# A weight chunk's float64 words handled at 1024 columns instead of twice 512, with an instruction order worked out anew

## The chip, the cores and the metric

The kernel runs on one core of one Trainium2 chip. The metric is the device time of one execution in microseconds (us). Five engines work side by side: TensorE (PE, matrix products), VectorE (DVE), ScalarE (ACT), GpSimd (POOL) and SyncE (SP, which issues the transfers). Each takes its instructions in the order in which they stand in its own queue, and waits at an instruction until what that one reads is there.

## The reference

Linear attention with random features, then two feed-forward layers, in single precision; the weights arrive as float64.

```
# attention: batch 4, heads 8, seq 576, head_dim 64, 128 features
h   = x @ omega.T - sum(x*x)/2           # x = q*s or k*s, s = 64**-0.25
phi = exp(h - max(h)) / sqrt(128)
kv  = einsum('bhsm,bhsd->bhmd', phi(k), v);  z = sum(phi(k))
a   = (phi(q) @ kv) / (phi(q) . z + 1e-6)
# x = a as [2304 tokens, 512]
xn  = x / sqrt(mean(x*x) + 1e-6) * rms_g
g   = xn @ w_gate                        # [512, 1536]
y   = (g*sigmoid(g) * (xn @ w_val)) @ w_out     # [1536, 512]
h   = y @ w_in                           # [512, 2048]
out = where(h > 0, h, exp(min(h, 0)) - 1) @ w_out2   # [2048, 512]
```

## The kernel before

**Work and tiles.** All products in the feed-forward layers run on pairs of 16-bit numbers: each operand is split into a high and a low part, and three matmuls of 128x256 replace one. The 2304 tokens are 9 blocks of 256, and a block is two query tiles of 128 (query tiles 6 and 7 are block 3, 8 and 9 block 4). `k_job` takes one of 20 key tiles through the feature map `phi` into the sums of its batch; `q_job` takes one of 18 query tiles through `phi`, a transposing transfer, 24 small matmuls with the sums (128x65 in the trace, the attention product), the division, the norm, the split and another transposing transfer. What comes out is the tile's *x*: the right-hand operand of `moe1_pair`, whose matmuls (`RM,RW`, 128x256) can't start without it. `moe1_pair` and `moe1_out` are the first feed-forward layer of one block, `moe2_quad` and `moe2_out` the second.

**Weights.** `Conv` (line 675) brings a chunk of 128 x 1024 float64 numbers on chip and turns it into float32 with integer steps. There are 34 chunks: 6 each of wg (`w_gate`), wv (`w_val`) and wo (`w_out`), 8 of w1 (`w_in`) and 8 of w2 (the second `w_out`). `load` issues two transfers, one per half of the chunk, into raw buffers of 512 columns x 2 words. `words` makes three results out of each half: the size without its sign from the upper word (ACT, or DVE, as the planner chooses), the top bits of the lower word (POOL, or DVE), and the sign bit (always DVE, on 16-bit numbers). `fp32` then finds the largest value of the chunk over all 1024 columns at once, and for each half joins the parts with a shift-and-or (DVE). Then the chunk's largest exponent over all partitions is needed: `spread` has PE turn a column of 128 maxima into a row (a matmul `RI,RS` of 1x128), DVE reduces it, and a second small matmul (`RS,RI`) hands it to all partitions. `split` scales and splits into high and low part. `spread` is used as well for each query tile and for each block's result (*the exponent* of a tile, a block or a chunk below). For w1 `conv_cols` does this 8 times with one buffer set `cv2`; w2 goes through DRAM first (`conv_store`, then `conv_forms`). wg, wv and wo use the set `cv`, which lies in RX (the arena that later holds the first layer's results): four raw halves, four halves for the sign and low bits, and three wide results. `cv2` and w2's set have two raw halves and two of the other kind, in RA.

**The order.** Nothing is issued as it is written. A `Plan` records every instruction with a cost, works out due times backwards from the two layers' products (the *spine*, whose order on PE is given), and then places the instructions one after the other on the five engines. The queues hold what it worked out, in that order. Where a step can go to two or three engines (`plan.choose`), the cheapest by its own costs gets it. The numbers at the head of the file bend this: `BIAS` shifts the due times of one job each (0 to 37 the key and query tiles, 38 to 43 the chunks of wg and wv, 44 to 56 wo, 57 w1, 58 the store of w2, 60 its forms, 61 the second layer), `PRICE` the choice of engine, `AHEAD`, `BLIM`, `PELEAD`, `INFL`, `LEAD` and `STRETCH` how early things are taken. As `Plan` issues all, each row of the trace names line 530; rows are told apart by their tiles: RA and RX work buffers and weights under way, RW the weights of the first layer, RM x and the blocks' temporaries, RS single columns, RI the unit matrix and the ones of `spread`, ps the banks of PSUM, w the weights w1 and w2 in DRAM, f the DRAM buffers for w2.

Of the kernel before, what the change touches and what calls it, by code (L numbers as in the profile page):

```python
# [7 lines left out]
F32 = mybir.dt.float32  # L8
F16 = mybir.dt.float16
I32 = mybir.dt.int32  # L10
U32 = mybir.dt.uint32
U16 = mybir.dt.uint16
BF16 = mybir.dt.bfloat16
AF = mybir.ActivationFunctionType
ALU = mybir.AluOpType
# [9 lines left out]
TPE = 1  # L25
KV32 = 2
HALF = 2
AHEAD, BLIM = 1540580.623, 6
QPE = 3
FINE = 9  # L30
BIAS = [1, -22, 0, -12, 8, 10, 1, -7, -6, 14, 26, 7, 0, 2, -36, -40, 59, 0, 26, -23, 0, -36, 41, -65, -115, 60, 0, -2, -73, -72, 0, -47, -43, -15, 226, -101, -257, -27, 0, 11, -9, -26, 15, 25, 55, 0, 3, 53, -60, 1, -17, 1, 102, 7, 7, -1, 0, 28, -17, 3, 56, 56]
LOOK, WEIGH = 0.076, 80
PRICE = [2.561, 1.313, 0.814, 2.417, 0.6, 0.917]
PELEAD = 127543.557
INFL, LEAD = 1.668, 51.224
STRETCH = (11.923, 880.565, 0.234)
NBLK = NT // NB
EXPM = 0x7F800000
SGN = -(1 << 31)
# [100 lines left out]
class Plan:  # L140
# [7 lines left out]
    SPAN = 3.4133  # L148
    SPARE = {"B": 2, "L": 2, "M": 2}
    FIRST = range(38, 57)  # L150
# [154 lines left out]
    def deadlines(self):  # L305
        at = 0.0
        for op in self.ops:
            op.due = 1e9
            if op.spine:
                op.due = at  # L310
                at += op.cost * (STRETCH[0] if at < STRETCH[1] else STRETCH[2])
        for op in reversed(self.ops):
# [3 lines left out]
    def order(self, limit=None):  # L316
        for op in self.ops:
            op.due -= BIAS[op.job] * (not op.spine)
        left = [len(op.deps) for op in self.ops]
# [85 lines left out]
        while True:  # L405
# [134 lines left out]
def fused(ctx: ExitStack, tc: tile.TileContext, qT, kT, kTt, qn, kn, v, v1, omT, eye, g, wg, wv, wo, w1, w2, out):  # L540
    nc = tc.nc
    plan = Plan()
    vec, act, pool, pe, sp = [plan.engine(n, e) for n, e in (("DVE", nc.vector), ("ACT", nc.scalar), ("POOL", nc.gpsimd), ("PE", nc.tensor), ("SP", nc.sync))]
# [60 lines left out]
    in_r, d_r, e_r, qp_r = Dyn("L", [1024], F32), Dyn("L", [1024], F32), Dyn("L", [2, 1024], F16), Dyn("L", [16, P], F16)  # L604
    x_r, xs_r, S_r = Dyn("M", [512], F32), Dyn("M", [2, 512], F16), Dyn("M", [8, P], F16)

# [9 lines left out]
    isi, e2, so2 = tt([8]), tt([8]), tt([8])  # L616
# [58 lines left out]
    class Conv:  # L675


        def __init__(self, raw, A, M):
            self.raw = Rot([a.view(o, [512, 2], I32) for a, o in raw])
            self.A = Rot([a.view(o, [512], I32) for a, o in A])  # L680
            self.M = Rot([a.view(o, [1024], F32) for a, o in M])

        def load(self, st, src):
            st["raw"] = [self.raw.next(), self.raw.next()]
            n = src.shape[1] // 2
            for i, r in enumerate(st["raw"]):
                sp.dma_start(out=r.rearrange("p (k f) w -> p k (f w)", k=n), in_=src[:, i * n:(i + 1) * n])

        def words(self, st):


            if "M" not in st:
                st["M"] = self.M.next()
            M = st["M"]
            st["A"] = [self.A.next(), self.A.next()]
            for i, (r, A) in enumerate(zip(st["raw"], st["A"])):
                Mi = M[:, 512 * i:512 * i + 512]
                plan.choose(lambda: act.activation(out=Mi, in_=r[:, :, 1].bitcast(F32), func=AF.Abs),
                            lambda: vec.tensor_scalar(out=Mi.bitcast(I32), in0=r[:, :, 1], scalar1=0x7FFFFFFF, scalar2=None, op0=ALU.bitwise_and))
                A16 = A.bitcast(U16).rearrange("p (f w) -> p f w", w=2)  # L700
                r16 = r.rearrange("p f w -> p (f w)").bitcast(U16).rearrange("p (f w) -> p f w", w=4)
                plan.choose(lambda: pool.tensor_scalar(out=A, in0=r[:, :, 0].bitcast(U32), scalar1=2.0 ** -29 * (1.0 - 2.0 ** -10), scalar2=-0.4995, op0=ALU.mult, op1=ALU.add),
                            lambda: vec.tensor_scalar(out=A16[:, :, 0], in0=r16[:, :, 1], scalar1=13, scalar2=None, op0=ALU.logical_shift_right))
                vec.tensor_scalar(out=A16[:, :, 1], in0=r16[:, :, 3], scalar1=0x8000, scalar2=None, op0=ALU.bitwise_and)

        def fp32(self, st, mcol):

            M = st["M"]
            vec.tensor_scalar(out=M, in0=M, scalar1=65536.0, scalar2=2.0, op0=ALU.mult, op1=ALU.max, accum_out=mcol)
            for i, A in enumerate(st["A"]):  # L710
                Mi = M[:, 512 * i:512 * i + 512].bitcast(I32)
                vec.scalar_tensor_tensor(out=Mi, in0=Mi, scalar=3, in1=A, op0=ALU.logical_shift_left, op1=ALU.bitwise_or)

        def split(self, st, hi, lo, s, parts=1):

# [22 lines left out]
    def src_rows(w, j):  # L738
        return w.rearrange("(k p) f -> p k f", p=P)[:, 2 * j:2 * j + 2, :]
# [33 lines left out]
    def conv_store(cv, w, e):  # L773

        for j in range(8):
            st = {}
            cv.load(st, src_rows(w, j))
            cv.words(st)
            cv.fp32(st, e[:, j:j + 1])
            sp.dma_start(out=f2[j], in_=st["M"])  # L780
# [62 lines left out]
    def setup_consts():  # L843
        sp.dma_start(out=om[0:64], in_=omT)
        sp.dma_start(out=om2[64:128], in_=omT)
        sp.dma_start(out=idn, in_=eye)
        sp.dma_start(out=gx, in_=g.partition_broadcast(P))
        vec.tensor_scalar(out=om[0:64], in0=om[0:64], scalar1=cc, scalar2=None, op0=ALU.mult)
        vec.memset(om[64:128], -cc * cc / 2.0)
        vec.tensor_scalar(out=om2[64:128], in0=om2[64:128], scalar1=cc, scalar2=None, op0=ALU.mult)  # L850
        vec.memset(om2[0:64], -cc * cc / 2.0)
        vec.memset(mh, -0.5)
        m, m_, mg = sm(1, "m1"), sm(1, "m1b"), sm(1, "mg")
        vec.memset(m, 1e-30)
        vec.tensor_reduce(out=m[0:64], in_=om[0:64], op=ALU.max, axis=AX.X, apply_absolute_value=True)
        vec.memset(ones, 1.0)
        vec.tensor_scalar(out=m_, in0=spread(m, 1), scalar1=1e-30, scalar2=None, op0=ALU.max)
        iw = sm(1, "iw")
        s = pow2(m_, 12, iw)
        for a in (0, 64):  # L860
            act.activation(out=Wh[a:a + 64], in_=om[0:64], func=AF.Copy, scale=s[0:64])
            vec.scalar_tensor_tensor(out=Wl[a:a + 64], in0=om[0:64], scalar=s[0:64], in1=Wh[0:64], op0=ALU.mult, op1=ALU.subtract)
        vec.tensor_copy(out=kap0, in_=iw)
        vec.tensor_reduce(out=mg, in_=gx, op=ALU.max, axis=AX.X, apply_absolute_value=True)
        vec.tensor_scalar(out=mg, in0=mg, scalar1=1e-30, scalar2=None, op0=ALU.max)
        s = pow2(mg, -1, gpow)
        vec.tensor_scalar(out=gx, in0=gx, scalar1=s, scalar2=None, op0=ALU.mult)
# [457 lines left out]
        plan.job = 59  # L1325

    setup_consts()
    cv = Conv([(RX, i * 4096) for i in range(4)], [(RX, 16384 + i * 2048) for i in range(4)], [(RX, 24576 + i * 4096) for i in range(3)])

    def wo_scales():  # L1330
        ih = sm(6, "ih")
# [10 lines left out]
    for t in range(2 * NBLK):  # L1342
        if t % 2 == 0 and t // 2 >= 2:
            i = t // 2 - 2
# [21 lines left out]
        q_job(t, key)  # L1366
        plan.job = 59
        key += 1
    cv2 = Conv([(RA, 32768), (RA, 36864)], [(RA, 40960 + i * 2048) for i in range(2)], [(RA, 45056 + i * 4096) for i in range(3)])
    room = Rot([RA.view(o, [1024], F32) for o in (45056, 49152, 53248, 32768, 36864)] + [RM.view(28672, [1024], F32)])  # L1370
    plan.job = 58
    conv_store(Conv([(RA, 34816), (RA, 38912)], [(RA, 43008), (RA, 45056)], [(RA, 47104)]), w2, e2)
    plan.job = 57
    for j in range(8):
        conv_cols(cv2, [(w1, WI)], j, isi[:, j:j + 1])
# [69 lines left out]
```

## Time and profile before

| | |
|---|---|
| median of 3 runs | 987.38 us (986.22 to 987.43) |
| the profiled execution | 987.1 us |
| its span in the trace | 985.3 us |
| PE, DVE, ACT, POOL busy in the span | 93%, 67%, 55%, 63% |
| mean granted clock of PE | 0.972 of full speed |

The time is that of the whole execution, the span runs from the first to the last instruction of the trace; 1.8 us lie around it. A share of busy time is a mean over stages with different limits. So a reader looks at the stages one by one: which engine is nearly always busy there, and, where PE idles, which event ended its wait. The granted clock falls where PE has idled and rises again later, so an idle microsecond of PE can cost more than itself.

### The profile page before, as it was taken

To read this page: it belongs to the slowest core of one execution; us is meant where nothing else is said; L and a number is where in the kernel's file an instruction comes from. 1 tells how busy PE (TensorE), PEld (TensorE's weight loads), DVE (VectorE), ACT (ScalarE), POOL (GpSimd) and SP (SyncE) were. 2 spreads that over 40 slices of the span, in tenths; PEclk is the share of its full clock that TensorE was granted. 3 is DMA by queue.
4 is the path that set the end of the run, shared out by engine and by line. 5 is a ranking of instruction groups with operands and counts; after the bars stand their busy time and mean duration, and the time that the engine had idled before them with its cause. 6 is when DMAs were issued, how large, how long until landed. Compare 5 with 4: busy or idle time off the path is not lost. (4 is left out here: it accounts for less than half of the span.)

```text
span 985.3 us, 22369 instructions
## 1 busy us (share of the span) xinstructions
PE 919.1 (93%) x8904; PEld 808.2 (82%) x8904; DVE 662.1 (67%) x1618; ACT 541.7 (55%) x1014; POOL 621.6 (63%) x676
## 2 busy tenths in 40 slices
PE   6486789999989999999999999999999999999998
PEld 5386678788878878888887778888888888888887
DVE  6876899856678775768985886377626475365642
ACT  6886554625556756664643456777535564354630
POOL 2669766856969688788664568999515264152630
PEclk9587899999999999999999999999999999999999
DMA  9954554123331252124765433100000000000001
GB/s 260 231 155 142 161 173 169 28 55 87 76 87 55 66 108 71 33 77 140 187 220 130 137 120 108 65 1 7 12 23 12 12 12 17 18 17 12 12 12 43
DMA packets 82567, 82.57 MB, mean 84 GB/s; under 512 B 52896, under 2 KB 57888, under 8 KB 82464
## 3 DMA queue, kind: packets, MB, share of 16 engines
q1 hardware_dynamic: 82464, 81.16, 29.6%
q8 instruction: 69, 1.13, 0.5%
q14 instruction: 34, 0.28, 0.1%
HBM read 59.90 MB, written 8.91 MB: 70 GB/s over the span
## 5 line engine op out<-in xcount | busy, mean ns | idle before, releaser
L530 PEld LDWEIGHTS <-RW 128*128 128x128 f16 x4864 | 457.7, 99 | 79.3 <-issue 16.4
L530 PE MATMUL ps<-RM,RW 128*128 128x256 f16 (+1 forms) x3240 | 369.1, 272 | 5.7 <-POOL RW L530 2.4
L530 PEld LDWEIGHTS <-RA 128*128 128x128 f16 (+2 forms) x2984 | 257.6, 98 | 33.5 <-issue 3.6
L530 PE MATMUL ps<-RX,RA 128*128 128x256 f16 x1728 | 196.3, 273 | 1.3 <-DVE RM L530 1.2
L530 POOL TENSOR_TENSOR RA<-RA 64x512 f16<-64x512 f32 (+4 forms) x108 | 144.9, 1343 | 40.0 <-ACT RA L530 14.5
L530 ACT ACTIVATE RM<-ps,RC 128x512 f32<-128x512 f32 (+1 forms) x135 | 90.0, 669 | 103.1 <-PE ps L530 66.4
L530 ACT ACTIVATE RM<-RM 128x512 f32<-128x512 f32 (+3 forms) x166 | 98.1, 594 | 39.2 <-DVE RM L530 34.3
L530 DVE SCALAR_TENSOR_TENSOR ps<-ps,RM 128x512 f32<-128x512 f32 x72 | 50.2, 697 | 91.7 <-POOL RM L530 91.6
L530 POOL TENSOR_SCALAR RM<-RM,RC 128x512 f32<-128x512 f32 x72 | 55.3, 768 | 84.9 <-ACT RM L530 84.4
L530 POOL TENSOR_TENSOR RM<-RM 128x512 f16<-128x512 f32 (+1 forms) x97 | 95.7, 994 | 12.5 <-ACT RM L530 6.6
L530 DVE TENSOR_REDUCE RS<-ps 128x4 f32<-128x512 f32 (+5 forms) x146 | 75.0, 536 | 36.4 <-PE ps L530 36.0
L530 PE MATMUL ps<-RX,RW 128*128 128x256 f16 x864 | 98.5, 273 | 0.2 <-DVE RA L530 0.2
L530 ACT ACTIVATE RA<-RA 128x512 f32<-128x512 f32 (+3 forms) x88 | 66.7, 769 | 56.3 <-DVE RA L530 19.9
L530 DVE SCALAR_TENSOR_TENSOR RM<-RM,ps 128x512 f32<-128x512 f32 x108 | 73.0, 680 | 36.2 <-ACT RM L530 25.0
L530 POOL TENSOR_TENSOR RW<-RM,RW 128x256 f16<-128x256 f32 (+1 forms) x67 | 48.1, 727 | 39.3 <-ACT RW L530 24.8
L530 PE MATMUL ps<-RW 128*128 128x256 f16 x600 | 71.7, 273 | 0.9 <-DVE RM L530 0.9
L530 ACT ACTIVATE RA<-RA,RS 64x512 f16<-64x512 f32 (+3 forms) x71 | 53.0, 758 | 29.9 <-POOL RS L530 19.5
L530 PE MATMUL ps<-RW,RA 128*128 128x256 f16 (+2 forms) x560 | 67.0, 273 | 1.2 <-DVE RM L530 1.2
L530 POOL TENSOR_SCALAR RA<-RA,RS 64x512 f32<-64x512 f32 (+3 forms) x67 | 48.3, 721 | 24.9 <-ACT RA L530 21.4
L530 DVE TENSOR_TENSOR RM<-ps,RM 128x256 f32<-128x256 f32 x108 | 45.0, 420 | 10.5 <-ACT RM L530 6.2
L530 POOL TENSOR_SCALAR RX<-RX 128x512 int32<-128x512 uint32 x36 | 26.7, 742 | 40.1 <-DMA RX<-wg 13.9
L530 DVE SCALAR_TENSOR_TENSOR RM<-ps,RC,RM 128x256 f32<-128x256 f32 x54 | 25.1, 478 | 39.6 <-PE ps L530 35.7
(143 smaller groups left out, 1194.7 us busy)
## 6 DMA issues: line engine op xcount, KB each, us to landing
RA<-w SPq DMA_DIRECT2D x32, 512.0 KB, 4.0
RX<-wg SPq DMA_DIRECT2D x12, 512.0 KB, 5.2
RX<-wv SPq DMA_DIRECT2D x12, 512.0 KB, 6.0
RX<-wo SPq DMA_DIRECT2D x12, 512.0 KB, 4.9
out<-RM SPq DMA_DIRECT2D x36, 128.0 KB, 1.7
f<-RA SPq DMA_DIRECT2D x8, 512.0 KB, 3.0
RA<-f SPq DMA_DIRECT2D x8, 512.0 KB, 3.3
RA<-qn SPq DMA_DIRECT2D x11, 256.0 KB, 3.0
```

The lines of the kernel that those rows point to most:

```text
L530: getattr(real, fn)(*[fix(x) for x in a], **{i: fix(x) for i, x in k.items()})
```

## The change

`Conv` no longer works in halves. A raw buffer holds 1024 columns x 2 words, and each step of `words` and the shift-and-or of `fp32` is one instruction over 1024 columns. The transfers stay two of half a chunk each, into one buffer. The bytes of the buffers stay the same: `cv` now has two whole raw buffers and two whole ones of the other kind, `cv2` and w2's set one of each.

```diff
-AHEAD, BLIM = 1540580.623, 6
+AHEAD, BLIM = 2665473.472, 7
...
-PRICE = [2.561, 1.313, 0.814, 2.417, 0.6, 0.917]
+PRICE = [2.61, 1.246, 0.912, 2.233, 0.537, 1.098]
...
-            self.raw = Rot([a.view(o, [512, 2], I32) for a, o in raw])
-            self.A = Rot([a.view(o, [512], I32) for a, o in A])
+            self.raw = Rot([a.view(o, [1024, 2], I32) for a, o in raw])
+            self.A = Rot([a.view(o, [1024], I32) for a, o in A])
...
-            st["raw"] = [self.raw.next(), self.raw.next()]
-            n = src.shape[1] // 2
-            for i, r in enumerate(st["raw"]):
-                sp.dma_start(out=r.rearrange("p (k f) w -> p k (f w)", k=n), in_=src[:, i * n:(i + 1) * n])
+            st["raw"] = self.raw.next()
+            n = src.shape[1]
+            r = st["raw"].rearrange("p (k f) w -> p k (f w)", k=n)
+            for i in range(2):
+                c = slice(i * n // 2, (i + 1) * n // 2)
+                sp.dma_start(out=r[:, c], in_=src[:, c])
...
-            st["A"] = [self.A.next(), self.A.next()]
-            for i, (r, A) in enumerate(zip(st["raw"], st["A"])):
-                Mi = M[:, 512 * i:512 * i + 512]
-                plan.choose(lambda: act.activation(out=Mi, in_=r[:, :, 1].bitcast(F32), func=AF.Abs),
...
+            M, r = st["M"], st["raw"]
+            A = st["A"] = self.A.next()
+            plan.choose(lambda: act.activation(out=M, in_=r[:, :, 1].bitcast(F32), func=AF.Abs),
...
-            for i, A in enumerate(st["A"]):
-                Mi = M[:, 512 * i:512 * i + 512].bitcast(I32)
-                vec.scalar_tensor_tensor(out=Mi, in0=Mi, scalar=3, in1=A, op0=ALU.logical_shift_left, op1=ALU.bitwise_or)
+            Mi = M.bitcast(I32)
+            vec.scalar_tensor_tensor(out=Mi, in0=Mi, scalar=3, in1=st["A"], op0=ALU.logical_shift_left, op1=ALU.bitwise_or)
...
-    cv = Conv([(RX, i * 4096) for i in range(4)], [(RX, 16384 + i * 2048) for i in range(4)], [(RX, 24576 + i * 4096) for i in range(3)])
+    cv = Conv([(RX, i * 8192) for i in range(2)], [(RX, 16384 + i * 4096) for i in range(2)], [(RX, 24576 + i * 4096) for i in range(3)])
...
-    cv2 = Conv([(RA, 32768), (RA, 36864)], [(RA, 40960 + i * 2048) for i in range(2)], [(RA, 45056 + i * 4096) for i in range(3)])
+    cv2 = Conv([(RA, 32768)], [(RA, 40960)], [(RA, 45056 + i * 4096) for i in range(3)])
...
-    conv_store(Conv([(RA, 34816), (RA, 38912)], [(RA, 43008), (RA, 45056)], [(RA, 47104)]), w2, e2)
+    conv_store(Conv([(RA, 34816)], [(RA, 43008)], [(RA, 47104)]), w2, e2)
```

All the other numbers of the planner change too, nearly every one of `BIAS`. In the instruction streams DVE has 1536 instructions where it had 1584, ACT 962 where it had 995, POOL 613 where it had 672, and PE the same 8696. DVE has 263 to 276 `tensor_tensor`, since 13 subtractions went there from POOL. PE's order differs in the first half and is nearly the same from the second layer on.

The head of SP's queue before, where kT is the first key tiles, omT the attention's omega and qT the first query tile:

```order
L530 DMA RW<-kT 64x1024
L530 DMA RO<-omT 64x128
L530 DMA RC<-omT 64x128
L530 DMA RW<-kTt 64x512
L530 DMA RW<-kT 64x1024
L530 DMA RX<-wg 128x2x512 x2
L530 DMA RX<-wv 128x2x512 x2
L530 DMA RI<-eye 128x128
```

And now:

```order
L530 DMA RX<-wg 128x2x512 x2
L530 DMA RX<-wv 128x2x512 x2
L530 DMA RW<-kT 64x1024
L530 DMA RO<-omT 64x128
L530 DMA RC<-omT 64x128
L530 DMA RW<-kTt 64x512
L530 DMA RI<-eye 128x128
L530 DMA RW<-qT 64x1024
```

The four transfers of the first wg and wv chunk moved ahead of the first key tile.

PE's queue before, where block 2's exponent is made (the two small matmuls) and the first product on block 3's x follows (the last row):

```order
L530 LDWEIGHTS RS
L530 MATMUL ps_65<-RI,RS 1x128
L530 LDWEIGHTS RI
L530 MATMUL ps_65<-RS,RI 128x1
L530 LDWEIGHTS RW
L530 MATMUL ps_68<-RM,RW 128x256
```

And now, the first small matmul with what stands around it:

```order
L530 MATMUL ps_62<-RM,RW 128x256
L530 LDWEIGHTS RS
L530 MATMUL ps_61<-RI,RS 1x128
L530 LDWEIGHTS RW
L530 MATMUL ps_62<-RM,RW 128x256
```

The second one stands 24 matmuls later. Between query tile 7's attention product and the first matmul on its x there stood 68 matmuls before, and 424 stand there now; for tile 9 these are 116 and 124.

SP's queue before, where the w1 and w2 chunks are loaded (`RA<-w`; the store of the last w2 chunk is `f_83<-RA`, and the transposes are those of late query tiles' x):

```order
L530 DMA RA<-w 128x2x512
L530 DMA f_83<-RA 128x1024
L530 DMA RA<-w 128x2x512
L530 DMA_TRANSPOSE RX<-RA 128x8x128
L530 DMA RA<-w 128x2x512
L530 DMA_TRANSPOSE RX<-RA 128x8x128
L530 DMA RA<-w 128x2x512 x13
```

And now:

```order
L530 DMA f_82<-RA 128x1024
L530 DMA_TRANSPOSE RX<-RA 128x8x128 x2
L530 DMA RA<-w 128x2x512
L530 DMA f_83<-RA 128x1024
L530 DMA_TRANSPOSE RX<-RA 128x8x128
L530 DMA RA<-w 128x2x512 x15
```

The loads of w1 stand behind the transposes now and follow one another. Between the small matmuls for the first and for the last of w1's eight exponents PE had 412 matmuls before and has 494 now.

## Rows read from the trace of the kernel before

**Rows 1.** Page: each engine's busy time, share of the span and instructions.

```profile
PE 919.1 (93%) x8904; PEld 808.2 (82%) x8904; DVE 662.1 (67%) x1618; ACT 541.7 (55%) x1014; POOL 621.6 (63%) x676
```

**Rows 2.** Stretches: length; PE, PEld, DVE, ACT, POOL busy (instructions); clock; DMA share, GB/s.

```profile
0.00:60.00 60.00, 35.01 (x219) 31.23 (x220) 41.71 (x114) 44.86 (x80) 29.30 (x37) 0.77 0.78 210
60.00:125.00 65.00, 48.95 (x526) 44.36 (x525) 52.25 (x140) 40.65 (x78) 52.48 (x58) 0.84 0.60 173
125.00:205.00 80.00, 74.14 (x740) 64.27 (x738) 70.59 (x135) 43.15 (x66) 59.06 (x52) 1.00 0.39 114
275.00:291.00 16.00, 12.61 (x123) 10.02 (x121) 11.29 (x39) 8.77 (x13) 11.54 (x10) 0.89 0.33 72
345.00:354.00 9.00, 7.04 (x72) 5.61 (x70) 6.59 (x26) 3.95 (x7) 7.71 (x9) 0.81 0.34 65
526.00:593.00 67.00, 61.01 (x538) 50.78 (x536) 51.96 (x138) 30.09 (x43) 38.77 (x36) 1.00 0.47 131
```

**Rows 3.** Chain of waits, its last long piece: start, length, what.

```profile
915.10 67.00 PE ps L530 x612
```

**Rows 4.** Groups by form: out<-in, count; busy us, mean ns; idle before and releasers.

```profile
L530 ACT ACTIVATE RX<-RX 128x512 f32<-128x512 f32 x27 | 18.1, 670 | 9.0 <-POOL RW L530 4.7 <-DMA RX<-wg 2.4 <-DMA RX<-wv 1.8
L530 ACT ACTIVATE RA<-RA 128x1024 f32<-128x1024 f32 x6 | 6.3, 1056 | 9.2 <-DVE RA L530 9.2
L530 DVE SCALAR_TENSOR_TENSOR RM<-RM,ps 128x512 f32<-128x512 f32 x108 | 73.0, 680 | 36.2 <-ACT RM L530 25.0 <-PE ps L530 10.2
L530 DVE SCALAR_TENSOR_TENSOR RM<-ps,RM 128x256 f32<-128x256 f32 x36 | 15.2, 423 | 1.1
L530 DVE TENSOR_SCALAR RA<-RA 128x512 uint16<-128x512 uint16 x32 | 18.2, 573 | 6.5 <-POOL RA L530 6.5
L530 DVE SCALAR_TENSOR_TENSOR RA<-RA 128x512 int32<-128x512 int32 x32 | 24.7, 803 | 0.2
L530 POOL TENSOR_SCALAR RA<-RA 128x512 int32<-128x512 uint32 x32 | 25.1, 785 | 35.9 <-DMA RA<-w 21.4 <-DVE RA L530 11.6 <-POOL RA L530 0.7
```

**Rows 5.** Timeline, 0 to 10 us: start, length, engine, instruction [idle before <-releaser].

```profile
3.90 1.10 SPq L530 DMA_DIRECT2D RX<-wg  x2
...
5.12 5.26 PE L530 MATMUL ps<-RO,RW 128*128 128x128 f32 x22 [5.12 <-ACT RW L530]
...
8.60 0.65 POOL L530 TENSOR_SCALAR RX<-RX 128x512 int32<-128x512 uint32 x1 [8.17 <-DMA RX<-wg]
...
9.28 0.46 DVE L530 TENSOR_SCALAR RX<-RX 128x512 uint16<-128x512 uint16 x1 [4.32 <-POOL RX L530]
```

**Rows 6.** Timeline, 272 to 290 us, PE and SP's queue, tile 7 and block 3.

```profile
272.35 0.90 PE L530 MATMUL ps<-RA,RX 128*128 128x65 f16 x24
...
280.43 1.23 SPq L530 DMA_TRANSPOSE RM<-RA  x1
280.82 0.22 PE L530 MATMUL ps<-RI,RS 128*1 128x128 f16 x1 [0.97 <-DVE RS L530]
...
283.62 1.99 PE L530 MATMUL ps<-RM,RW 128*128 128x256 f16 x12 [2.05 <-DMA RM<-RA]
```

**Rows 7.** Timeline, 345 to 353 us, PE, around block 3's exponent.

```profile
347.90 0.16 PE L530 MATMUL ps<-RS,RI 1*128 1x1 bf16 x1 [1.05 <-DVE RS L530]
...
349.16 1.61 PE L530 MATMUL ps<-RO,RA 128*128 128x128 f16 x14 [0.88 <-POOL RA L530]
```

**Rows 8.** Page: DMA issues of w1, w2 (KB, us to landing); timeline, w1's stage.

```profile
RA<-w SPq DMA_DIRECT2D x32, 512.0 KB, 4.0
...
538.32 0.22 PE L530 MATMUL ps<-RI,RS 128*1 128x128 f16 x1 [2.23 <-DVE RA L530]
...
559.05 1.12 POOL L530 TENSOR_SCALAR RA<-RA,RS 128x1024 f32<-128x1024 f32 x1 [3.54 <-ACT RA L530]
560.25 2.13 POOL L530 TENSOR_TENSOR RA<-RA 128x1024 f16<-128x1024 f32 x1
...
589.28 0.22 PE L530 MATMUL ps<-RI,RS 128*1 128x128 f16 x1 [0.63 <-DVE RA L530]
```

More of the change, by code (lines that the diff above doesn't have):

```diff
@@ L27 @@
 HALF = 2
-AHEAD, BLIM = 1540580.623, 6
+AHEAD, BLIM = 2665473.472, 7
 QPE = 3
 FINE = 9
-BIAS = [1, -22, 0, -12, 8, 10, 1, -7, -6, 14, 26, 7, 0, 2, -36, -40, 59, 0, 26, -23, 0, -36, 41, -65, -115, 60, 0, -2, -73, -72, 0, -47, -43, -15, 226, -101, -257, -27, 0, 11, -9, -26, 15, 25, 55, 0, 3, 53, -60, 1, -17, 1, 102, 7, 7, -1, 0, 28, -17, 3, 56, 56]
+BIAS = [0, -24, -6, -13, 9, 11, 1, -18, 4, 16, 26, 0, 3, 0, -42, -66, 48, 0, 24, -36, 11, -47, 60, -76, -82, 71, 3, 7, -74, -72, 7, -40, -68, -29, 214, -138, -2, -19, 6, 12, -10, -26, 30, 98, 29, -5, -6, 50, -58, 0, -29, 29, 0, 7, -28, 113, -9, 8, -23, 3, 1, 0]
 LOOK, WEIGH = 0.076, 80
-PRICE = [2.561, 1.313, 0.814, 2.417, 0.6, 0.917]
-PELEAD = 127543.557
-INFL, LEAD = 1.668, 51.224
-STRETCH = (11.923, 880.565, 0.234)
+PRICE = [2.61, 1.246, 0.912, 2.233, 0.537, 1.098]
+PELEAD = 228143.172
+INFL, LEAD = 1.815, 51.617
+STRETCH = (11.046, 890.942, 0.188)
 NBLK = NT // NB
@@ L693, in words @@
                 st["M"] = self.M.next()
-            M = st["M"]
-            st["A"] = [self.A.next(), self.A.next()]
-            for i, (r, A) in enumerate(zip(st["raw"], st["A"])):
-                Mi = M[:, 512 * i:512 * i + 512]
-                plan.choose(lambda: act.activation(out=Mi, in_=r[:, :, 1].bitcast(F32), func=AF.Abs),
[L699 to L704, printed above, removed]
+            M, r = st["M"], st["raw"]
+            A = st["A"] = self.A.next()
+            plan.choose(lambda: act.activation(out=M, in_=r[:, :, 1].bitcast(F32), func=AF.Abs),
+                        lambda: vec.tensor_scalar(out=M.bitcast(I32), in0=r[:, :, 1], scalar1=0x7FFFFFFF, scalar2=None, op0=ALU.bitwise_and))
+            A16 = A.bitcast(U16).rearrange("p (f w) -> p f w", w=2)
+            r16 = r.rearrange("p f w -> p (f w)").bitcast(U16).rearrange("p (f w) -> p f w", w=4)
+            plan.choose(lambda: pool.tensor_scalar(out=A, in0=r[:, :, 0].bitcast(U32), scalar1=2.0 ** -29 * (1.0 - 2.0 ** -10), scalar2=-0.4995, op0=ALU.mult, op1=ALU.add),
+                        lambda: vec.tensor_scalar(out=A16[:, :, 0], in0=r16[:, :, 1], scalar1=13, scalar2=None, op0=ALU.logical_shift_right))
+            vec.tensor_scalar(out=A16[:, :, 1], in0=r16[:, :, 3], scalar1=0x8000, scalar2=None, op0=ALU.bitwise_and)
         def fp32(self, st, mcol):
```

## The prediction

> **What bounds the kernel now.** I read the busy times of the engines first, then the stretches, then single waits of TensorE (PE). PE is busy 93% of the span [rows 1], so time can only be won where PE idles or runs at the low clock. The stretches [rows 2] show where that is. Up to 60 us PE is busy 35.0 of 60 at a granted clock of 0.77 on the mean (of its two levels, 1.2 and 2.4 GHz, the lower counts 0.5), up to 125 us 49.0 of 65 at 0.84, up to 205 us 74.1 of 80 at full clock: in these three stages VectorE (DVE) is busy 41.7, 52.3 and 70.6 us, so PE is fed by DVE there (with ScalarE, ACT, nearly as busy at first). After that PE is full, at about 67.0/612 = 0.1095 us for a 128x256 matmul [rows 3], but for three places. From 275 to 291 PE idles 16 - 12.6 = 3.4 us, and the clock granted falls to 0.89, some 1.4 us more (12.6 x 0.11): 4.8 us. From 345 to 354 it is 2.0 + 1.3 (7.04 x 0.19) = 3.3 us, and from 526 to 593, where w1 is converted, 6.0 us at full clock. These 14.1 us, and the first 205 us, are what the change can move. From 640 us on PE's order is nearly that of before, and I expect nothing there.
>
> **Fewer, longer instructions.** Each of 34 weight chunks loses one ACT, one GpSimd (POOL) and two DVE instructions. An ACT one of 512 columns takes 0.670 and of 1024 1.056 us [rows 4]: two halves 1.340, so 0.28 us less per chunk. For DVE's shift-and-or there is no row of 1024. The nearest rows are the two-input forms of 512 and 256 columns, 0.680 and 0.423 us [rows 4]: 0.257 per 256 columns, so 1.194 for 1024 against 2 x 0.680, 0.17 us less. For the 16-bit sign step there are only halves of 0.573 [rows 4]; the gain is between nothing and 0.3 us, and I take 0.1, near the other DVE form. POOL's step has a 1024-column relative of 1.12 us (another operation, with a scalar by pointer) against halves of 0.785 [rows 4, 8]: 0 to 0.4 us, I take 0.2. Only wg, wv and wo (18 chunks) are converted in the stage that DVE bounds: 18 x 0.27 = 4.9 us of DVE work. DVE is busy 164.6 of those 205 us, so 80% of it, 3.9 us, would shorten the stage if all the rest kept its place; the planner also hands DVE 13 subtractions from POOL (263 to 276 in the order). I take -3.0 us, with bounds -5 (all of it) and +1 (eaten by what POOL hands over). For w1 and w2 the work lies beside a full PE and is costed at nothing, except in the chain of chunks below.
>
> A row speaks of how long steps get in each other's way: the integer shift-and-or of 512 columns takes 0.803 us on the mean, the float form of the same size with one input in PSUM 0.680 [rows 4]. The Trainium skill, page "SBUF — State Buffer", section "Who interferes with whom", says that DVE instructions with two SBUF inputs lock the port pair shared with GpSimd for their whole length and the second comer fully blocks. By that rule a doubled instruction also doubles the longest wait, which would take back up to 34 x 0.12 = 4 us of POOL's and DVE's time; by the rows alone the total wait stays as it is. As POOL is not what PE waits for, both give the same sum here, and only the chain of w1 would feel it.
>
> **The start.** SP now issues the four loads of the first wg and wv chunk ahead of the first kT. In the trace the loads of kT at the queue's head let PE begin at 5.12 us, while the weight loads issued at 3.90 reach POOL at 8.60 and DVE at 9.28 [rows 5]: 4.7 us from issue to use. Issued at 0.7, the first chunk reaches POOL near 5.4, and whole (two more halves behind it, 1.4 to 2 us each) near 10; kT lands behind it, so PE begins at about 13 us, 8 us later. But DVE had nothing to do before 9.28 and now begins with the weights at about 8, so for the engine that bounds, I price it at +1.0 us: its first wait for PE. Ends: 0, and +5 if DVE runs dry until PE delivers.
>
> **Block 3's x.** At 283.62 PE waited 2.05 us for a transposing DMA, issued 3.2 us before at 280.43, of query tile 7; its attention product had ended at 272.35 + 0.90 [rows 6]. So the way from product to x takes 10.4 us, and PE had less work than that in between. In the order there stood 68 matmuls between that product and the first matmul on this x; now 424 stand there, some 40 us of work. The same spot holds PE's wait of 0.97 us for the block's exponent [rows 6]; its two small matmuls were neighbours and now have 24 matmuls between them. Both waits should go, and with them the low clock: -4.0 of 4.8 us, bounds -4.8 and -1 (something else is late there).
>
> **Block 4's x.** The waits of 1.05 and 0.88 us at 347.9 and 349.2 [rows 7] are of the same kind: the exponent's two matmuls side by side, and a late POOL step. The exponent's pair now has work between it, but query tile 9 gains only 8 matmuls of room (116 to 124), under 1 us. I take -2.3 of 3.3 us, bounds -3.3 and 0.
>
> **The chain of w1.** w1's chunks go through one raw buffer. Before, each half was refilled as soon as its own three readers were done; now both halves wait for the whole chunk. PE sits in this chain because each chunk's largest exponent goes through two small matmuls in its queue: it waited 2.23 us at 538.3, and the first to the last of these eight took 589.28 - 538.32 = 51.0 us [rows 8], 7.3 a chunk, while only 412 matmuls, 45.1 us, stood in between. Now 494 stand there, 54.1 us or 7.7 a chunk. The loop of a chunk is 0.7 to issue two halves, 4.0 to land [rows 8], 1.1 to 1.5 on POOL, 0.8 to 1.1 for the sign on DVE, 0.2 of signalling: 6.8 to 7.5 us. That is under 7.7, so most of the 6.0 us should go: -3.3. Bounds: -5 and, as below, +8.
>
> **New waits.** Another order has waits of its own that no row shows. Its tightest place that I find is query tile 13's x, with 12 us of matmuls where 15 stood, against the 10.4 us way above. I take +3.0, between 0 and +6 (half of the 14.1 us of the old places).
>
> **Sum.** -3.0 + 1.0 - 4.0 - 2.3 - 3.3 + 3.0 = -8.6 us. The profiled execution took 987.1 (span 985.3 and 1.8 around it), which gives 978.5; the median of the runs shown is 987.38, 0.3 above the profiled one, so I forecast 979 us.
>
> **The rivals.** First, new waits take the place of the old. PE is full only because the planner fits work to its costs; a late engine shows up elsewhere, and the trace has small waits all over 60 to 125 us. [...] Against it: the three places above have more room in the new order, counted. Then only the shorter instructions remain, some -1 us: 986.
>
> Second, slower, by the loop of w1: one buffer per chunk means that load, POOL, DVE and the next load follow one another with nothing beside. If each of the seven loops also waits behind one of POOL's long pairs of 1.12 + 2.13 us [rows 8], it takes 7.2 + 3.25 = 10.4 us, 2.7 over the 7.7 that stand in the order: 7 x 2.7 = 19 us lost where 6 were, +13 in place of -3.3, so 979 + 16 = 995. It decides from a loop of 9.9 us on, where the total reaches +2. The Trainium skill, page "Trainium Kernel Development and Optimization", section "Best Practices", asks for double buffering so that transfers run beside compute; this change takes halves that served as two buffers away at w1 and w2, and by that rule this rival is the outcome. Before, the measured 7.3 us a chunk was no better than my 6.8 to 7.5 for the whole chunk, which is against it.
>
> Third, the start costs its 8 us in full, because ACT and DVE find nothing else while kT is late: 979 + 7 = 986.
>
> Fourth, a larger gain: all places at their better ends and no new waits, 969 to 973.
>
> **Chances.** The forecast, taken as 974 to 984, 0.45; the first rival 0.20; the second 0.14; the third 0.11; the fourth 0.10. The range must leave out no more than 2 in 10: it runs from 969 to 990 and leaves the second rival and the edges of the others. A difference under 0.2%, 2 us, is about what a measurement of this kernel can't tell from no change. Faster by more: the forecast, the fourth, and a third of the first and third, 0.65. Within it: 0.17, the rest of the first and third, less 0.04 that land above. Slower: 0.14 + 0.04 = 0.18.
>
> **What would show it.** In the trace after, ACT, POOL and DVE show the weight steps at 1024 columns near 1.06, 1.2, 0.9 and 1.2 us; PE begins at about 13 us, and DVE has caught up by 60 us. Near the place of 283 us PE has no wait for a transposing DMA and the clock stays at its upper level, and the exponent's waits are gone. The eight exponent matmuls of w1 span about 54 us, with PE waiting under 2.5 us among them. I am wrong if PE at 205 us has done less than now, if those eight span over 60 us, or if as much waiting as went stands at other places between 205 and 526 us.

## The result, and the profile after

The changed kernel takes 977.45 us (median of 4 runs, 974.59 to 977.84) where the kernel before takes 987.40 (986.22 to 987.55): 0.9897 of it, 95% interval 0.9879 to 0.9914. That is some 10 us faster; 979 us were forecast. The profiled execution is the lowest of the four, 974.59 us with a span of 972.8.

Two rows of the profile after answer to [rows 1] and [rows 3]; the first gives each engine's busy time, share and instructions, the second is the last long piece of the chain of waits, after which PE has nothing more to do.

```profile
PE 911.0 (94%) x8904; PEld 802.7 (83%) x8904; DVE 667.1 (69%) x1570; ACT 537.7 (55%) x981; POOL 599.8 (62%) x617
```

```profile
902.52 67.05 PE ps L530 x612
```

DVE has 48 instructions less and is 5 us busier; the time has not come from less work on that engine alone. The stretches of the changed kernel have the columns of [rows 2]: length; PE, PEld, DVE, ACT, POOL busy; clock; DMA.

```profile
0.00:60.00 60.00, 30.77 (x214) 27.51 (x215) 47.57 (x112) 44.96 (x76) 31.60 (x33) 0.86 0.78 225
60.00:125.00 65.00, 52.37 (x596) 48.29 (x594) 55.70 (x127) 40.69 (x77) 53.83 (x50) 0.89 0.67 183
125.00:205.00 80.00, 73.76 (x715) 64.22 (x713) 66.14 (x121) 42.48 (x58) 63.95 (x50) 0.94 0.34 105
...
275.00:291.00 16.00, 16.00 (x205) 13.90 (x203) 13.73 (x36) 9.47 (x12) 8.80 (x7) 1.00 0.13 38
291.00:354.00 63.00, 62.93 (x690) 54.87 (x690) 45.51 (x116) 37.59 (x72) 48.59 (x46) 1.00 0.28 63
354.00:526.00 172.00, 168.43 (x1807) 147.55 (x1804) 121.55 (x286) 97.16 (x166) 124.29 (x112) 1.00 0.45 124
526.00:593.00 67.00, 64.91 (x578) 54.86 (x576) 57.12 (x137) 33.51 (x43) 29.12 (x22) 1.00 0.41 140
```

One stretch of the kernel before, as it is not among [rows 2]:

```profile
354.00:526.00 172.00, 171.84 (x1859) 151.54 (x1857) 129.52 (x295) 99.36 (x179) 129.48 (x129) 1.00 0.44 123
```

The places of 283 and 347 us are full at full clock now, w1's stage has 64.91 busy us where it had 61.01, and 354 to 526 us, which had been full, has 3.6 idle us. Busy time at a changing clock is hard to add up. So the next table counts work: each matmul that has ended by a time, at what its shape takes at full clock in the trace (0.109 us for 128x256), 873.3 us in all in either kernel. What a stage is longer than the work done in it is lost there; the end is that of PE's last matmul, 982.1 us before and 969.6 after. "Again" is the same changed kernel, profiled once more in the experiments.

| stage, us | before | after | after, again |
|---|---|---|---|
| 0 to 60 | 38.3 | 38.9 | 38.0 |
| 60 to 125 | 25.5 | 19.6 | 20.4 |
| 125 to 205 | 8.3 | 10.1 | 9.7 |
| 205 to 275 | 2.9 | 2.9 | 2.9 |
| 275 to 291 | 6.0 | 0.8 | 1.0 |
| 291 to 354 | 6.4 | 3.0 | 2.7 |
| 354 to 526 | 4.3 | 8.4 | 8.9 |
| 526 to 640 | 11.6 | 7.1 | 7.7 |
| 640 to PE's end | 5.4 | 5.4 | 6.1 |
| sum | 108.7 | 96.2 | 97.4 |

The widened steps, in the groups by form (count, busy us, mean ns), first as halves before, then as they are after:

```profile
L530 DVE TENSOR_SCALAR RX<-RX 128x512 uint16<-128x512 uint16 x36 | 19.1, 563 | 4.9 <-POOL RX L530 4.9
L530 DVE SCALAR_TENSOR_TENSOR RX<-RX 128x512 int32<-128x512 int32 x24 | 17.9, 768 | 0.1
L530 DVE SCALAR_TENSOR_TENSOR RW<-RW,RX 128x512 int32<-128x512 int32 x12 | 10.9, 934 | 0.0
```

```profile
L530 POOL TENSOR_SCALAR RX<-RX 128x1024 int32<-128x1024 uint32 x18 | 22.0, 1221 | 19.3 <-DVE RC L530 6.8 <-DMA RX<-wg 5.9 <-DVE RI L530 3.5
L530 DVE SCALAR_TENSOR_TENSOR RA<-RA 128x1024 int32<-128x1024 int32 x16 | 20.0, 1252 | 0.2
L530 DVE TENSOR_SCALAR RX<-RX 128x1024 uint16<-128x1024 uint16 x18 | 16.3, 904 | 3.4 <-POOL RX L530 3.4
L530 DVE SCALAR_TENSOR_TENSOR RX<-RX 128x1024 int32<-128x1024 int32 x12 | 16.0, 1334 | 0.1
L530 ACT ACTIVATE RX<-RX 128x1024 f32<-128x1024 f32 x14 | 15.7, 1125 | 11.9 <-DVE RX L530 7.8 <-POOL RW L530 3.3 <-DMA RX<-wv 0.7
L530 DVE SCALAR_TENSOR_TENSOR RW<-RW,RX 128x1024 int32<-128x1024 int32 x6 | 9.5, 1586 | 0.1
```

For wg, wv and wo DVE's two steps fell from 19.1 + 17.9 + 10.9 = 47.9 to 16.3 + 16.0 + 9.5 = 41.8 us: 6.1 us less, 4.9 were forecast. By these means two shift-ors of 512 columns cost 0.35 us more than one of 1024 (2 x 0.803 - 1.252, w1 and w2). But a mean also counts the instructions that were held up. Where nothing held them, two halves in a row took 1.29 us before and a whole one 1.23 after, 0.06 us apart:

```profile
538.29 1.29 DVE L530 SCALAR_TENSOR_TENSOR RA<-RA 128x512 int32<-128x512 int32 x2
```

```profile
524.03 1.23 DVE L530 SCALAR_TENSOR_TENSOR RA<-RA 128x1024 int32<-128x1024 int32 x1
```

So, where the two halves follow each other, only a small part of the difference is a fixed cost of each instruction. Summed over the single instructions of wg's, wv's and wo's steps on DVE, what exceeds the shortest of the same group is 10.5 us before and 7.1 after: 3.4 of the 6.1 us are less of such holding up.

### The profile page after: what moved, and what is told of

It is laid out like the page before. It is cut to its first block, busy times and chain, and to the rows that moved or that the text cites. A ratio compares the mean times of both kernels' runs of the same rounds, so it can differ in the third digit from the quotient of the medians.

```text
span 972.8 us, 22167 instructions
## 1 busy us (share of the span) xinstructions
PE 911.0 (94%) x8904; PEld 802.7 (83%) x8904; DVE 667.1 (69%) x1570; ACT 537.7 (55%) x981; POOL 599.8 (62%) x617
## 5 line engine op out<-in xcount | busy, mean ns | idle before, releaser
L530 PEld LDWEIGHTS <-RW 128*128 128x128 f16 x4800 | 451.7, 98 | 69.0 <-issue 12.2
L530 PE MATMUL ps<-RM,RW 128*128 128x256 f16 (+1 forms) x3240 | 365.4, 271 | 5.0 <-ACT RA L530 3.1
L530 PEld LDWEIGHTS <-RA 128*128 128x128 f16 (+3 forms) x3128 | 261.0, 98 | 31.5 <-issue 1.8
L530 POOL TENSOR_TENSOR RA<-RA 64x512 f16<-64x512 f32 (+6 forms) x91 | 122.6, 1349 | 22.8 <-DVE RS L530 4.9
L530 POOL TENSOR_TENSOR RM<-RM 128x512 f16<-128x512 f32 (+1 forms) x94 | 100.9, 1077 | 42.0 <-ACT RM L530 36.2
L530 POOL TENSOR_SCALAR RM<-RM,RC 128x512 f32<-128x512 f32 x72 | 57.7, 802 | 93.6 <-ACT RM L530 93.5
L530 DVE TENSOR_REDUCE RS<-ps 128x4 f32<-128x512 f32 (+5 forms) x146 | 75.4, 536 | 27.6 <-PE ps L530 26.9
L530 DVE SCALAR_TENSOR_TENSOR RM<-RM,ps 128x512 f32<-128x512 f32 x108 | 73.2, 681 | 26.8 <-ACT RM L530 17.9
L530 ACT ACTIVATE RA<-RA 128x1024 f32<-128x1024 f32 (+5 forms) x69 | 61.3, 897 | 49.8 <-DVE RA L530 12.8
L530 ACT ACTIVATE RA<-RA,RS 64x512 f16<-64x512 f32 (+3 forms) x69 | 51.7, 759 | 27.3 <-POOL RS L530 11.3
L530 POOL TENSOR_TENSOR RW<-RM,RW 128x256 f16<-128x256 f32 (+1 forms) x63 | 43.7, 704 | 34.4 <-ACT RW L530 18.5
L530 POOL TENSOR_SCALAR RA<-RA,RS 64x512 f32<-64x512 f32 (+2 forms) x63 | 43.9, 697 | 22.2 <-ACT RA L530 15.8
L530 POOL TENSOR_TENSOR RA<-RM,RA 128x256 f16<-128x256 f32 (+1 forms) x50 | 34.4, 696 | 32.1 <-ACT RA L530 21.0
```

The source lines that it names most:

```text
L530: getattr(real, fn)(*[fix(x) for x in a], **{i: fix(x) for i, x in k.items()})
```

## The experiments

Twelve runs in three groups; each group ran on a chip of its own, and ratios are against the kernel before on that chip (medians of 991.0, 989.3 and 989.2 us). A ratio is estimated from all executions and is not the quotient of two medians; a difference between medians of two groups is one between two chips as well. Where moved steps need code of their own, the trace's line numbers are a little higher (531 to 536).

### The widths, with the order kept

In three runs every widened step is recorded as before and stands at its place in its queue, but is issued in pieces:

```diff
         for real, fn, a, k in op.calls:
...
+            k = {i: fix(x) for i, x in k.items()}
+            if getattr(op, "wide", False) and op.job in HALVED:
+                for c in (slice(0, 512), slice(512, 1024)):
+                    getattr(real, fn)(**{i: x[:, c] if isinstance(x, bass.AP) else x for i, x in k.items()})
+                continue
...
```

> The changed kernel with its order kept instruction by instruction, but every widened step (sign-free size, low bits, sign bit, shift-and-or) of all 34 chunks issued as two instructions of 512 columns in the same place of the same queue. Theory W (the shorter instructions bring about 3 us, in the first 205 us, where DVE bounds): 977.4 + 3.0 = 980.4, between 979 and 983. Theory O (the order alone brings all of the 10 us): 977.4, within 1 us. If the widths brought all of it: 987. Beside the total, the loss of PE up to 205 us should grow by about 3 us and the stage of w1 stay within 1 us.

> As the run with halves everywhere, but only the 18 chunks of wg, wv and wo are in halves. Theory W: all of the 3 us is here, 980.4. If the gain of the widths lies in the chain of w1 instead: 977.4.

> As the run with halves everywhere, but only the 16 chunks of w1 and w2 are in halves. Theory W: PE is full there and 54 us of its work stand between the first and the last of the eight exponents, so 977.4, within 1 us. Rival: the chain of a chunk decides; a chunk in halves takes 0.25 us longer on POOL's, 0.25 on DVE's and 0.2 on ACT's part, so up to 7 x 0.7 = 5 us more, 982.

Measured: 980.52 us (0.9908, 0.9876 to 0.9939) everywhere, 979.59 (0.9896, 0.9863 to 0.9929) for wg, wv and wo, 978.20 (0.9877, 0.9845 to 0.9910) for w1 and w2. The changed kernel itself, in the next group:

> The changed kernel itself, for comparison on the same chip as the others: about 1.0% under the kernel before. The three runs with halves stand at 0.990, 0.990 and 0.988 of the kernel before on their chip; if the changed kernel stands at 0.990 here, the halves cost nothing that can be seen; if at 0.987, theory W holds.

Measured: 976.63 us (0.9866, 0.9836 to 0.9896). So the halves cost 3.9, 3.0 and 1.6 us between the medians, in the order that theory W wants and of its size, but the intervals overlap. Two things stand beside this. With all steps in halves the new order still keeps two thirds of what the changed kernel gains (0.9908 against 0.9866), so most of the gain is the order's. And the stage does not fit: by the count of work the two profiled executions with wg, wv and wo in halves had lost only 0.4 to 1.0 us more than the changed kernel at 205 us, where 3 were expected; the rest came later. As the medians alone don't settle it, the suspected cost was tripled:

```diff
-                for c in (slice(0, 512), slice(512, 1024)):
+                for c in [slice(256 * i, 256 * i + 256) for i in range(4)]:
```

> The changed kernel's order again, but the widened steps of the 18 chunks of wg, wv and wo in four pieces of 256 columns: the suspected cost tripled, since two pieces add one instruction to each step and four add three. Theory W: three times what the halves cost there (3.0 us between the medians), 9 us: 986, between 983 and 990. If the width is of no weight beside the order: 977.4, within 1.5 us.

Measured: 988.20 us (0.9986, 0.9967 to 1.0005), 11.6 us over the changed kernel's 976.63, and the intervals of the two ratios are far apart. The number of pieces counts. Where it counts is told by wo's exponent, the one matmul with RI and RC (128x6) that all of wo's scaling waits for; the timelines of PE in the changed kernel and in the one with quarters:

```profile
166.25 0.22 PE L530 MATMUL ps<-RI,RC 128*6 128x128 f16 x1
```

```profile
176.94 0.22 PE L536 MATMUL ps<-RI,RC 128*6 128x128 f16 x1 [1.16 <-DVE RW L536]
```

It comes 10.7 us later. This profiled execution was 3.1 us slower than the median of its run, and its span is 16.7 and 15.5 us over the two of the changed kernel; so the 10.7 are about two thirds of its loss. By the count of work the quarters lose 62.8 us up to 125 (the changed kernel 58.5 and 58.4) and 18.0 from 125 to 205 (10.1 and 9.7): of what they lose more by 205 us, two thirds lie in the stage where wo is converted. DVE's groups for wg, wv and wo, with halves there and then with quarters:

```profile
L534 DVE SCALAR_TENSOR_TENSOR RX<-RX 128x512 int32<-128x512 int32 x24 | 20.5, 892 | 0.1
L534 DVE TENSOR_SCALAR RX<-RX 128x512 uint16<-128x512 uint16 x36 | 20.1, 601 | 4.6 <-POOL RX L534 4.6
L534 DVE SCALAR_TENSOR_TENSOR RW<-RW,RX 128x512 int32<-128x512 int32 x12 | 12.1, 1047 | 0.0
```

```profile
L534 DVE TENSOR_SCALAR RX<-RX 128x256 uint16<-128x256 uint16 x72 | 31.2, 500 | 3.5 <-POOL RX L534 3.5
L534 DVE SCALAR_TENSOR_TENSOR RX<-RX 128x256 int32<-128x256 int32 x48 | 23.3, 543 | 0.1
L534 DVE SCALAR_TENSOR_TENSOR RW<-RW,RX 128x256 int32<-128x256 int32 x24 | 11.5, 534 | 0.0
```

They take 52.7 and 66.0 us in place of 41.8, in the same order; what exceeds the shortest of each group sums to 16.1 and 24.8 us, where it was 7.1.

### The planner's numbers alone

> The widened steps with the planner's numbers of before, so that the planner works out another order from them. If the numbers only fine-tune: 984 (before less the 3 us of the shorter instructions). If an order is only as good as the numbers that were fitted to just these costs, the waits come back: slower than before, 990 to 1000.

Measured: 1041.96 us (1.0522, 1.0491 to 1.0554). That is far slower than either theory said. Two stretches of it, same columns as above:

```profile
205.00:245.00 40.00, 26.10 (x296) 22.45 (x294) 29.44 (x85) 23.10 (x40) 23.45 (x23) 0.79 0.35 73
...
354.00:412.00 58.00, 39.12 (x421) 32.32 (x419) 40.71 (x131) 32.85 (x64) 46.48 (x46) 0.79 0.42 90
```

PE idles 14 and 19 us there, at a low clock (0.79), behind late transposes and steps of POOL and DVE on query tiles. The widened steps with the numbers that were fitted to halves lose 51 us against the kernel before on that chip: these numbers don't serve for other costs. That does not make the widths the gain: in the new order most of it stays when the steps are issued in halves. The other half, halves in the plan with the new numbers, has no run, since from these the planner works out no complete order.

### Block 3's late x, taken out of the order before

The prediction valued the place of 283 us at 4 us. In three runs of the kernel before, steps there were moved within their queues and nothing else; each step n goes right ahead of step m:

```diff
+        for n, m in MOVES:
+            op = self.ops[n]
+            ops.remove(op)
+            ops.insert(ops.index(self.ops[m]), op)
```

> The kernel before with one thing of the new order: the two small matmuls of block 2's exponent, which stood side by side ahead of the first product on block 3's x, now stand behind its first 12 and 24 matmuls. Theory: PE's two waits there (0.97 and 0.37 us) go, but the x lands when it did, so its wait grows by as much: no change, within 0.5 us. Rival: the waits add up, 1.3 us and some of the low clock faster, 985.5.

Measured: 1.0012 (0.9989 to 1.0034). The interval, some 2 us to either side, just leaves out the rival's 985.5 (a ratio of 0.9981) and is too wide to show half a microsecond. In the trace, as expected, the wait for x took over what the exponent had cost (2.05 + 0.97 + 0.37 us before); PE's timeline:

```profile
285.88 1.51 PE L531 MATMUL ps<-RM,RW 128*128 128x256 f16 x7 [3.73 <-DMA RM<-RA]
```

> The kernel before with the same, and query tile 7's attention product two groups of 12 matmuls earlier and its six DVE steps ahead of a neighbour's, so that its x lands some 2.9 us earlier. Theory (the place of 283 us is one late x): of 3.4 us of idle PE 2.5 go, and the low clock of 1.4 us with it: 3.5 us faster, 983.5. Rival: PE's time comes back as waits within the next 60 us: no change.

Measured: 1.0006 (0.9984 to 1.0029), but the x had not come earlier, so this run tells nothing of its price. The timeline of all engines shows why:

```profile
274.21 2.12 POOL L531 TENSOR_TENSOR RA<-RA 128x1024 f16<-128x1024 f32 x1 [1.17 <-ACT RA L531]
...
274.85 1.51 DVE L531 TENSOR_SCALAR RS<-RS,RC 128x8 f32<-128x8 f32 x1
...
287.04 1.65 PE L531 MATMUL ps<-RM,RW 128*128 128x256 f16 x12 [3.44 <-DMA RM<-RA]
```

A DVE step on 8 columns of that chain took 1.51 us: it ended together with the POOL subtraction that had begun at 274.21. The next step then found ACT's queue taken. So in the third run the whole way was moved, on all queues:

> The kernel before with all of query tile 7's way from product to x brought forward: besides the product two groups of 12 matmuls earlier, its DVE, ACT and POOL steps stand ahead of their neighbours on each queue and of tile 8's subtraction on POOL, and the exponent's matmuls behind the first products on block 3's x. In the run before this the x had not come earlier, since POOL held one of the DVE steps for 1.5 us and ACT's queue the next. Now it should land some 3.5 us earlier and PE's idle time between 275 and 291 us fall from 3.4 us under 1. Theory (one late x costs what PE idles there and the low clock): 0.996 of the kernel before, 4 us faster. Rival (given back within the next 80 us): 1.000.

Measured: 1.0012 (0.9995 to 1.0029). This time the place itself is cured. The stretches of the run with the exponent alone, then of this one:

```profile
275.00:291.00 16.00, 12.27 (x116) 9.75 (x113) 9.65 (x30) 7.63 (x10) 10.20 (x11) 0.89 0.40 83
291.00:354.00 63.00, 59.47 (x710) 51.48 (x708) 46.71 (x132) 39.22 (x72) 47.21 (x47) 1.00 0.26 63
...
526.00:593.00 67.00, 63.16 (x557) 52.44 (x556) 52.99 (x136) 31.88 (x47) 39.06 (x37) 1.00 0.46 135
```

```profile
275.00:291.00 16.00, 14.59 (x155) 12.17 (x152) 10.34 (x35) 4.89 (x7) 11.55 (x10) 1.00 0.36 80
291.00:354.00 63.00, 58.20 (x686) 50.37 (x682) 46.05 (x128) 41.72 (x74) 47.71 (x46) 1.00 0.25 63
...
526.00:593.00 67.00, 62.18 (x536) 51.31 (x534) 50.49 (x130) 30.55 (x45) 36.37 (x35) 0.97 0.49 135
```

Between 275 and 291 us PE is 2.3 us busier and the clock stays up: 3.6 us won by the count of work (2.5 lost against 6.1). Then PE idles 1.3 us more up to 354 and 1.0 more in w1's stage, and counted up to 593 us both have lost the same since 275 within half a microsecond (27.9 and 27.6 us). The rival holds for this place: what PE won there was lost again at the next ones, and the total excludes the theory's 0.996.

### The start

> The changed kernel with the first key tile's loads ahead of the first wg and wv chunk on SP, its square ahead of the weights on ACT, its matmuls first on PE (at about 5 us instead of 12.3) and three of its DVE steps in the time in which DVE has nothing yet. Theory (DVE bounds the start, so PE's first 7 us are worth little): within 1.5 us of the changed kernel's 977. Rival (the late start costs PE's 7 us): 970 to 972.

Measured: 978.88 us (0.9892, 0.9862 to 0.9922), 2.2 over the changed kernel between the medians. PE's timelines, here and in the changed kernel:

```profile
5.37 3.78 PE L531 MATMUL ps<-RO,RW 128*128 128x128 f32 x16 [5.37 <-ACT RW L531]
15.71 0.27 PE L531 MATMUL ps<-RI,RS 128*2 128x128 f16 x1 [6.56 <-DVE RX L531]
17.92 0.16 PE L531 MATMUL ps<-RI 2*128 2x2 bf16 x1 [1.94 <-DVE RI L531]
```

```profile
12.26 0.26 PE L530 MATMUL ps<-RI,RS 128*2 128x128 f16 x1 [12.26 <-DVE RX L530]
```

PE begins 6.9 us earlier and then waits 6.56 and 1.94 us for DVE's weight steps, which are 3.4 us later. Starting PE earlier in this way brought nothing; as the loads of the weights stand behind those of the key tile then, the run does not give the price of PE's late start by itself.

### The largest new wait

The longest of the changed kernel's new waits had not been foreseen. A timeline of DVE, ACT and PE:

```profile
140.81 1.11 ACT L530 ACTIVATE RW<-RX 128x1024 f32<-128x1024 f32 x1 [0.96 <-DMA RX<-wo]
141.95 1.22 DVE L530 TENSOR_SCALAR_CACHE_REDUCE RW<-RW 128x1024 f32<-128x1024 f32 x1 [1.09 <-ACT RW L530]
...
143.28 0.27 DVE L530 TENSOR_REDUCE RS<-ps 1x1 bf16<-1x128 f32 x1
...
143.60 0.16 PE L530 MATMUL ps<-RS,RI 1*128 1x1 bf16 x1 [6.03 <-DVE RS L530]
```

PE waits 6.03 us for a small reduction whose input had been ready, and which stands in DVE's queue behind a step on a wo chunk. Two runs moved it:

```diff
+MOVES = [(1103, 1132), (429, 1132)]
```

> The changed kernel with two small DVE steps moved (the reduction of a key tile's exponent and that of a wo/wv chunk's, which stand behind a wide step on a wo chunk that waits for ACT): they now stand 10 places earlier on DVE, and PE's wait of 6.0 us at 143.6 us should shrink under 1.5 us. Theory A: PE's waits add up, so all of it and the low clock after it come back: 977.4 - 7 = 970. Theory B: in this stage wo's conversion is the bound, and the first product that needs it (1.9 us of slack at 192.4 us) takes the rest back: 975.5.

Measured: 978.03 us (0.9887, 0.9857 to 0.9917), no faster than the changed kernel. The wait fell to 0.75 us, and PE had lost 4.5 us less at 150 us (63.0 against 67.5), but then it met this:

```profile
138.42 0.16 PE L531 MATMUL ps<-RS,RI 1*128 1x1 bf16 x1 [0.75 <-DVE RS L531]
...
166.22 0.27 PE L531 MATMUL ps<-RI,RC 128*6 128x128 f16 x1 [4.21 <-DVE RW L531]
```

It is the same matmul on wo's exponent that the quarters delayed, at the same time as ever (166.22 and 166.25). So what was won at 143.6 us went again at this matmul, as theory B says. By 180 us PE had lost 70.9 us, 3.0 more than without the move; what took these 3.0 no run shows.

> The changed kernel with the two moved DVE steps of the run on key tile 19's exponent and, besides, wo's conversion brought forward: a POOL step on its chunk 3 (which stood 9 us in POOL's queue while its data lay ready) 9 us earlier, so that the raw buffer is free and the last chunk loaded 8 us earlier, and the steps behind it on all queues moved up accordingly. Theory B (wo's conversion bounds the stage from 125 to 205 us): now PE keeps the 4.5 us that it had won at 150 us in that run, 972 to 974. If the stage's bound is the sum of DVE's or POOL's work: no gain, 977.

Measured: 986.64 us (0.9971, 0.9947 to 0.9995), 10 us slower than the changed kernel. The last wo chunk's largest value was ready at 162.5 instead of 166.2 us, but the matmul on it did not come earlier:

```profile
169.01 0.22 PE L531 MATMUL ps<-RI,RC 128*6 128x128 f16 x1 [3.52 <-DVE RM L531]
```

Its wait is ended by a DVE step on another tile, and PE waits there for DVE twice more (2.35 and 3.06 us), with some forty steps moved. That the stage waits for wo's conversion is supported by the quarters and by the run before; this run, in which the conversion came forward and other steps late, neither confirms it nor speaks against it.

## Why the prediction was right, and where it was not

**Sum.** 979 was forecast, 977.45 measured. By the table the terms came out so (forecast, then after and, in brackets, the second profile):

| step | forecast | measured |
|---|---|---|
| widths and start, 0 to 205 us | -3.0 + 1.0 | -3.5 (-4.0) |
| block 3's x, 275 to 291 | -4.0 | -5.2 (-5.0) |
| block 4's x, 291 to 354 | -2.3 | -3.4 (-3.7) |
| chain of w1, 526 to 640 | -3.3 | -4.5 (-3.9) |
| new waits, 354 to 526 | +3.0 | +4.1 (+4.6) |

Every term has the sign that was forecast, and each came out 1.1 to 1.5 us larger (0.6 to 2.0 by the second profile). Together they give -12.5, since the profiled run was 2.9 us under the median; the second profile gives -11.3.

**Fewer, longer instructions.** The size of -3.0 us is borne out: 3.0 with halves, within the scatter, and 11.6 with quarters, of which a third is 3.9. The working behind it is not, so that the agreement is in part luck. By the means the single sizes were low: the sign step saves 0.22 us a chunk instead of 0.1, the shift-or 0.20 to 0.35 instead of 0.17, POOL's 0.26 to 0.40 instead of 0.2 (ACT's saves 0.22 instead of 0.28). But the means hold waits; two undisturbed half shift-ors in a row take only 0.06 us more than a whole one. And the share was wrong: not 80% of DVE's time shortens the stage, but a quarter to a half of it (3.0 of 10.9 us with halves, 11.6 of 24.2 with quarters). The two errors cancelled. The reason given, that DVE bounds up to 205 us by its sum of work, is the step that failed: in the changed kernel DVE is busy for 169.4 of these 205 us, where it was 164.6, and still PE has lost 3.5 us less at their end. From 60 to 125 us, where 5.9 us were won, pieces cost little (20.8 lost with quarters against 19.6 and 20.4): that gain is the order's and was not in the sum. With quarters most is lost where wo's chunks follow one another and PE waits for the last one.

**The start.** PE began at 12.26 us, about 13 was said. By 60 us PE has lost 0.6 us more than before, or 0.3 less by the second profile, so the price was near the lower end; what the widths won in the same 60 us is not told apart from it. The third rival is out: nothing like 7 us is lost there.

**Block 3's and block 4's x.** In the changed kernel PE is busy without a break from 275 to 291 us, at full clock, and the waits for the exponent and for the transpose are gone. But the price of the place was read as if it stood alone. The runs on the order before show that it doesn't: cured in that order, block 3's brings nothing. In the changed kernel 8.6 us went at the two places and 4.1 came back between 354 and 526 us, which the sum held as new waits of +3.0 without knowing where. The tightest place named, query tile 13's x, is one of them:

```profile
454.56 1.70 PE L530 MATMUL ps<-RX,RW 128*128 128x256 f16 x14 [1.43 <-DMA RX<-RA]
```

So the first rival's mechanism is real. It did not decide: against the 8.6 us won at the two places 4.1 were lost after them. Why the new order kept the other half, where the order before kept nothing, no run shows; that this term of the sum came out is therefore in part luck too.

**The chain of w1.** The eight exponents' first matmuls stand from 523.99 to 581.76 us, a span of 57.8 (54 was forecast, over 60 would have been wrong), with one wait above 1 us:

```profile
523.99 0.22 PE L530 MATMUL ps<-RI,RS 128*1 128x128 f16 x1
533.57 0.22 PE L530 MATMUL ps<-RI,RS 128*1 128x128 f16 x1 [1.18 <-DVE RA L530]
...
581.76 0.22 PE L530 MATMUL ps<-RI,RS 128*1 128x128 f16 x1
```

That is 8.3 us a chunk, more than the 7.7 of the 494 matmuls and than the loop of 6.8 to 7.5 us, of which 0.2 for signalling stands in no row. But PE hardly waited for it, so the second rival, the slower loop with one buffer, did not come. (It would have decided from 9.6 us a chunk on, not 9.9: 979 + 7 x 1.9 - 6.0 + 3.3 is 2 us over the kernel before.) The Trainium skill's advice on double buffering in "Trainium Kernel Development and Optimization", section "Best Practices", by which that rival was to be the outcome, is not borne out at this place. Whether a second buffer would be faster still is not shown: in the run with w1's and w2's steps in halves (978.20 against 976.63) the two loads of a chunk were issued 0.5 us apart in nearly every chunk, as with whole steps.

**Locks.** The section "Who interferes with whom" of the Trainium skill's page "SBUF — State Buffer" names waits between GpSimd and DVE instructions with two SBUF inputs. The trace has long rows of such instructions, such as the shift-or of 3.00 us below. The prediction's choice was between waits that double with the width, up to 4 us, and a total that stays. Neither came: with fewer, longer instructions the excess over the shortest fell (10.5 to 7.1 us), and with quarters it rose to 24.8. That POOL is behind all of it is not shown.

## What to carry to other kernels

What an idle place of the bounding engine shows in a trace is not yet what its cure brings: three such places were taken out one by one here, the time did not change, and PE waited at later places instead. When the length of some steps is doubled in a kernel whose order is worked out from costs, fit the order to the new costs in the same change: the widened steps under the old numbers were 5% slower. To find out what the number of instructions of a step is worth, keep the order and cut the steps in four; two pieces were hardly above the scatter. And look beside the mean of a group at a row that nothing held up: half of what the widths saved on DVE was waiting, not length.

## What had not been expected of the hardware

A DVE step on 8 columns can take as long as a POOL subtraction of 1024 beside it, and both end together. The first two rows are from the kernel before; the second pair is from the one after, where a shift-or of 1024 columns took 3.00 us instead of its group's mean of 1.59 while POOL worked through four subtractions.

```profile
270.80 2.13 POOL L530 TENSOR_TENSOR RA<-RA 128x1024 f16<-128x1024 f32 x1 [1.17 <-ACT RA L530]
270.81 2.14 DVE L530 TENSOR_SCALAR RS<-RS 128x8 f32<-128x8 f32 x1
```

```profile
177.27 9.87 POOL L530 TENSOR_TENSOR RW<-RX,RW 128x1024 f16<-128x1024 f32 x4
...
182.15 3.00 DVE L530 SCALAR_TENSOR_TENSOR RW<-RW,RX 128x1024 int32<-128x1024 int32 x1
```
